# Values in an RWKV-6 kernel: 64 queries with 64 keys for half of the heads, in quarters of the matmul array, and the output's halves by the parity of the pair of heads

## The chip, the cores and the metric

The kernel runs on one core of one Trainium2 chip. The metric is the device time of one execution in microseconds. Five engines work side by side from queues of their own: TensorE (PE, matmuls), VectorE (DVE), ScalarE (ACT), GpSimd (POOL) and SyncE (SP), whose queue issues DMAs.

## The reference

An attention block with a decaying state, and behind it a feed-forward block. All data are float32.

```python
# r, k, v, w: (B=4, H=8, S=768, D=48); u: (H, D)
for t in range(S):
    cur = einsum('bhd,bhe->bhde', u * k[t], v[t])
    y[:, :, t] = einsum('bhd,bhde->bhe', r[t], state + cur)
    state = w[t][..., None] * state + einsum('bhd,bhe->bhde', k[t], v[t])
x = y.transpose(0, 2, 1, 3).reshape(B * S, H * D)       # (3072, 384)
h = x @ w_in                                            # (3072, 2048)
out = (h / (1 + exp(-h))) @ w_out                       # (3072, 384)
```

An output of the attention block is causal: token t takes the state and the keys up to its own, t. In a block of tokens it is therefore a sum of two products: the queries (with the decay up to them) with the state ahead of the block, and the values of the block weighted by scores, which are zero for keys behind the query.

## The kernel before, in words

The sequence is cut into 6 blocks of L = 128 tokens and the batch of 4 into 2 halves of NB = 2. A block with one half of the batch is a unit; there are 12, and they are worked through in order. The 8 heads are 4 pairs p (NP = 4): head 2p + e has its 48 channels in partitions 64 e to 64 e + 47. For the second member of a unit's batch, b = 1, keys and values stand in reversed order along the partitions, for b = 0 in order.

Scores are built in levels. At level l the block is cut into pieces of c = 2^l tokens, and queries of an odd piece meet keys of the even piece before it. `score_products` (L688 to L717) multiplies on TensorE, and VectorE (L722) or ScalarE (L801) puts the result into `score`, laid out as [key, e, b and pair, query]. The part within blocks of 8 tokens is put in by L577, in the units up to index 3 there is L604 for pairs of tokens in its place. The last level, l = 6, lets queries 64 to 127 meet keys 0 to 63. `grow_queries` and `grow_keys` multiply decays into queries and keys between levels.

When a unit's scores are finished, its output y comes from two functions that follow each other on TensorE. `y_state` (L835 to L845) multiplies the 48 x 48 state of each head with 128 queries: for each pair p, each b and each e one product, 16 in all, with rows 64 e of the array and output in partitions 64 b of one of two banks of PSUM, one bank for each e. `y_values` (L847 to L857) runs once for each e: for each p and b it multiplies the 128 x 48 values with the 128 keys by 128 queries of the scores and adds into the same place, 8 products for each e. ScalarE then copies each bank to `yt` in two copies, one for each b (L857). Units 0 and 1 use another function, `y`, which the change leaves alone; so `y_state` and `y_values` run for 10 units.

Behind it `update` (L879) adds the unit's keys and values to the state, and `move_x` moves `yt` by DMAs into `xt`, the layout that the feed-forward block reads. The feed-forward block of earlier units fills TensorE in between: `up` (L987, up-projection and Silu on ScalarE) and `quarter` (L1053, down-projection in seven products of half size by sums and differences that VectorE forms, L1035 and L1062).

The order is written out by hand. `mix` gives groups of attention steps for a unit; the loop at the end of the kernel puts some feed-forward steps behind each group, by the numbers in `room`. The last group of a unit holds the output step:

```python
[(y_state, i), *both(y_values, i), *both(update, i), *at(not ahead, (move_x, i))]
```

From unit 4 on, three up-projections stand between the last score products and this group. TensorE's instructions are in that order in one queue. A product's tile in the array follows from where its operands lie: the rows from the partitions of weights and moving data, the columns from the partitions of the output. A float32 product is carried out as two pairs of weight load and matmul instructions, one after the other in the compiled order.

Of the kernel before, what the change touches and what calls it, by code (L numbers as in the profile page):

```python
# [38 lines left out]
def kernel(  # L39
# [11 lines left out]
    nc = tc.nc  # L51

    B, H, S, D = r.shape
    DM, DF = moe_w_in.shape
    L = 128
    NL = 7
    NB = 2
    NP = H // 2
    PD = 64
# [24 lines left out]
    def bank(name, *dims):  # L84

        have = banks[name][turns_of[name] % 2][:]
        turns_of[name] += 1
        steps, n = [], 1
        for d in dims[::-1]:
            steps.insert(0, [n, d])  # L90
            n *= d
        return bass.AP(tensor=have.tensor, offset=have.offset, ap=[have.ap[0], *steps])
# [4 lines left out]
    vt, vq, whole = {}, {}, {}  # L97
# [191 lines left out]
    state = const.tile([128, B, NP, 2 * PD], F32, name="state")  # L289
# [43 lines left out]
    NSC = 1  # L333
    score = const.tile([128, NSC, 2, Q, L], F32, name="score")

    masks = {}
    first = {}
# [20 lines left out]
    tw, tr, tk, diag, kq, xt = {}, {}, {}, {}, {}, {}  # L358
# [112 lines left out]
    at = 768  # L471
# [358 lines left out]
    p_yt, p_kv, yt = {}, {}, {}  # L830
# [4 lines left out]
    def y_state(i):  # L835

        n, b0 = units[i]
        for e in range(2):
            p_yt[i, e] = bank("p_m", NP, L)
        for p in range(NP):  # L840
            for b in range(NB):
                for e in range(2):
                    rows = slice(PD * e, PD * e + D)
                    nc.tensor.matmul(p_yt[i, e][PD * b:PD * b + D, p, :], lhsT=state[rows, b0 + b, p, rows],  # L844
                                     rhs=tr[i][rows, b * NP + p, :], start=(p == 0), stop=False)  # L845

    def y_values(i, e):  # L847

        for p in range(NP):
            for b in range(NB):  # L850
                at = (2 * p + e) * D
                nc.tensor.matmul(p_yt[i, e][PD * b:PD * b + D, p, :], lhsT=whole[i][b][:, at:at + D],  # L852
                                 rhs=score[:, i % NSC, e, b * NP + p, :], start=False, stop=(p == NP - 1))
        if e == 0:
            yt[i] = pt.tile([128, NP, NB, L], F32, name="yt", bufs=1)
        for b in range(NB):
            nc.scalar.copy(out=yt[i][PD * e:PD * e + D, :, b, :], in_=p_yt[i, e][PD * b:PD * b + D])  # L857

    def y(i, b):

# [64 lines left out]
    def mix(i):  # L925
# [15 lines left out]
        def start(j):  # L941
            return [*[(product, j, l) for l in range(1, NL)], (grow_own, j, 1)]

        end = [[*at(ahead, *bonus_steps(i + 1, 0, 1, 2, 3))],
               [*at(i < len(units) - NB, (turn_apart, i), (turn_k, i)), *at(ahead, *turns(i + 1))],
               [(y_state, i), *both(y_values, i), *both(update, i), *at(not ahead, (move_x, i))]]
        if i < NPAIR:
            groups = [[*both(turn, i, "w"), (product, i, 0)],
# [188 lines left out]
    for m in range(6):  # L1137
# [8 lines left out]
    do((burst, 2, 5), (keep_level, 2, 5), (keep_level, 2, 6), (go_on, 2, 6), (bonus_write, 2), (up, 1, 6), (weight_sums, 1),  # L1146
       (load_values, 3), (turn_apart, 2), (turn_k, 2), (up, 1, 7), (weight_sums, 2), (sums, 1, 2))
    do((sums, 1, 3), (y_state, 2), *both(y_values, 2), *both(update, 2),
       (move_x, 2),
       *blocks[7:])  # L1150
# [44 lines left out]
```

## Time and profile before

| | |
|---|---|
| time, median of 3 runs | 603.54 us (603.06 to 603.57) |
| the profiled execution's own time | 603.03 us |
| its span, first to last instruction | 601.2 us |
| instructions | 15147 |
| matmul instructions | 5982, as many weight loads |
| granted TensorE clock | 1.0 throughout |
| product with the state, L844 | 320 matmul instructions, median 269 ns each |
| values, L852 | 320 matmul instructions, median 273 ns each |
| copies to yt, L857 | 40, median 580 ns each |

The time lies 1.8 us above the span: it takes in what is ahead of the first and behind the last instruction. A matmul's duration is its way from issue to the end of its writes, so matmuls that run behind each other or side by side overlap; what one costs is read from the distance of the starts. The chain that ended last is followed back from the last instruction: at each step to what released it, or to the instruction before it on its engine. "Issue" there is time in which the engine waited for nothing that the profile shows.

### The profile page before, as it was taken

What the parts mean: (1) busy time and instruction counts of PE and PEld (TensorE: products, weight loads), DVE (VectorE), ACT (ScalarE), POOL (GpSimd) and SP (SyncE); (2) the same over time, 40 slices, a digit from 0 to 9 for tenths busy, and PEclk for the clock granted to TensorE, in tenths of its full rate; (3) what the DMA queues carried; (4) which work ended last, traced back from release to release, by engine and by line L of the source; (5) the groups of instructions that cost most, each with busy time, mean ns of one, the idle gap of its engine ahead of it and who ended that gap; (6) DMA issues with size and microseconds to landing.
All of it is one profiled execution on the core that took longest, in us unless ns stands there. A gap on an engine that the chain in (4) does not pass through costs nothing.

```text
span 601.2 us, 15147 instructions
## 1 busy us (share of the span) xinstructions
PE 592.8 (99%) x5982; PEld 529.6 (88%) x5982; DVE 414.9 (69%) x709; ACT 232.5 (39%) x516; POOL 365.1 (61%) x414
## 2 busy tenths in 40 slices
PE   8999999999999999999999999999999999999997
PEld 7787876799899899889889889889889889889997
DVE  6879788798696695596695795686587587551041
ACT  6788883431530530530440351361351242250110
POOL 6998778257678668378578578478578567500000
PEclk9999999999999999999999999999999999999999
DMA  9957793343541643642643643643542531100000
GB/s 218 298 128 201 169 278 48 55 76 49 127 66 54 111 64 52 137 63 51 137 62 54 133 62 54 131 59 53 128 71 50 109 58 27 36 2 27 28 1 26
DMA packets 203079, 53.44 MB, mean 89 GB/s; under 512 B 186752, under 2 KB 194816, under 8 KB 203008
## 3 DMA queue, kind: packets, MB, share of 16 engines
q1 hardware_dynamic: 201424, 51.88, 42.1%
q8 instruction: 47, 0.77, 0.6%
q10 hardware_dynamic: 1584, 0.59, 0.4%
q14 instruction: 24, 0.20, 0.1%
HBM read 43.21 MB, written 5.24 MB: 81 GB/s over the span
## 4 chain that ended last, share of the span: by engine, by line
PE 87%; DVE 4%; POOL 3%; ACT 2%; DMA 1%; issue 1%; SPq 1%; DVEq 0%; POOLq 0%; ACTq 0%
PE p_h L987 38%; PE p_o L1053 34%; PE p_m L852 3%; PE p_m L1009 3%; PE p_sc L704 3%; PE p_m L704 2%; PE p_m L844 2%; POOL tk L645 1%; DMA u_bc<-in_u_dram 1%; DVE score L722 1%; PE p_sc L879 1%; POOL w_out_sb L255 1%; PE p_m L820 1%; POOL tw L422 1%; POOL w_in_sb L255 1%
## 5 line engine op out<-in xcount | busy, mean ns | idle before, releaser
L987 PE MATMUL p_h<-xt,w_in_sb 128*128 128x256 f32 x1152 | 258.9, 382 | 0.8 <-POOL tk L669 0.7
L987 PEld LDWEIGHTS p_h<-xt,w_in_sb 128*128 128x128 f32 x1152 | 215.8, 190 | 31.9 <-POOL tk L669 0.9
L996 ACT ACTIVATE gt<-p_h 128x512 f32<-128x512 f32 x90 | 53.5, 596 | 182.0 <-PE p_h L987 181.7
L645 POOL TENSOR_TENSOR tk<-tk,tw 128x256 f32<-128x256 f32 x128 | 94.2, 757 | 37.3 <-issue 21.4
L1053 PE MATMUL p_o<-own,temps 128*128 128x192 f32 x528 | 88.1, 326 | 0.0
L1053 PE MATMUL p_o<-w_out_sb,gt 128*128 128x192 f32 x508 | 87.4, 328 | 0.0
L1053 PEld LDWEIGHTS p_o<-own,temps 128*128 128x128 f32 x528 | 86.0, 190 | 0.3 <-DVE temps L1062 0.3
L507 POOL TENSOR_TENSOR ruk<-tokens_rk 128x768 f32<-128x768 f32 (+1 forms) x32 | 52.3, 1645 | 53.9 <-DMA tokens_rk<-in_k_dram 21.1
L1053 PEld LDWEIGHTS p_o<-w_out_sb,gt 128*128 128x128 f32 x508 | 82.7, 190 | 0.9 <-issue 0.4
L1035 DVE TENSOR_TENSOR temps<-gt 128x256 f32<-128x256 f32 x84 | 56.2, 669 | 22.4 <-ACT gt L996 22.4
L627 DVE TENSOR_TENSOR tr<-tr,tw 128x512 f32<-128x512 f32 x61 | 54.7, 896 | 16.3 <-PE p_m L704 12.6
L422 POOL TENSOR_TENSOR tw<-tw 128x256 f32<-128x256 f32 (+6 forms) x83 | 43.5, 524 | 36.5 <-DVE tw L374 32.5
L615 ACT COPY tk<-tk 128x256 f32<-128x256 f32 x52 | 21.0, 403 | 102.0 <-POOL tk L645 74.3
L722 DVE COPY_PREDICATED score<-mask,p_sc 128x512 f32<-128x512 int8 x42 | 31.2, 798 | 3.9 <-PE p_sc L704 3.7
L1062 DVE TENSOR_TENSOR temps<-p_o,partial 128x192 f32<-128x192 f32 x22 | 7.9, 358 | 36.1 <-PE p_o L1053 26.8
L1062 DVE TENSOR_TENSOR partial<-p_o,partial 128x192 f32<-128x192 f32 x33 | 11.7, 356 | 28.7 <-PE p_o L1053 28.7
L1035 DVE TENSOR_TENSOR temps<-temps,gt 128x256 f32<-128x256 f32 x43 | 30.4, 706 | 1.5
L1053 PE MATMUL p_o<-w_out_sb,temps 128*128 128x192 f32 x176 | 30.4, 326 | 0.0
L541 DVE TENSOR_REDUCE block_sums<-ruk 128x4 f32<-128x192 f32 (+1 forms) x48 | 24.2, 546 | 7.1 <-POOL ruk L507 7.1
L857 ACT COPY yt<-p_m 48x512 f32<-48x512 f32 x40 | 23.2, 580 | 14.9 <-PE p_m L852 10.1
L1053 PEld LDWEIGHTS p_o<-w_out_sb,temps 128*128 128x128 f32 x176 | 28.9, 190 | 0.0
L704 PEld LDWEIGHTS p_sc<-tr,tk 48*32 48x32 f32 (+1 forms) x1312 | 18.2, 119 | 11.1 <-issue 7.4
(187 smaller groups left out, 841.5 us busy)
## 6 DMA issues: line engine op xcount, KB each, us to landing
w_out_sb<-in_moe_w_in_dram SPq DMA_DIRECT2D x6, 768.0 KB, 6.8
w_out_sb<-in_moe_w_out_dram SPq DMA_DIRECT2D x4, 768.0 KB, 5.7
own<-in_moe_w_out_dram SPq DMA_DIRECT2D x4, 768.0 KB, 5.3
tokens_rk<-in_r_dram SPq DMA_DIRECT2D x8, 384.0 KB, 4.4
tokens_rk<-in_k_dram SPq DMA_DIRECT2D x8, 384.0 KB, 5.3
tokens_w<-in_w_dram SPq DMA_DIRECT2D x8, 384.0 KB, 6.4
xt<-yt SPq DMA_DIRECT2D x60, 48.0 KB, 2.0
raw<-in_w_dram SPq DMA_DIRECT2D x80, 32.0 KB, 1.9
```

Of the source, the lines that this page charges most:

```text
L422: engine.tensor_tensor(out=up, in0=t[:, :, 0::2], in1=t[:, :, 1::2], op=ALU.mult)
L507: mul = lambda out, one, two: nc.gpsimd.tensor_tensor(out=out, in0=one, in1=two, op=ALU.mult)
L541: add = lambda out, have: nc.vector.tensor_reduce(out=out, in_=have, axis=mybir.AxisListType.X, op=ALU.add)
L627: nc.vector.tensor_tensor(out=odd, in0=odd, in1=tw[i][l][:, :, 0::2][:, :, :, None].to_broadcast([128, Q, L >> (l + 1), c]), op=ALU.mult)
L645: nc.gpsimd.tensor_tensor(out=out, in0=have, in1=odd_products(i, l, b, *blocks), op=ALU.mult)
L704: nc.tensor.matmul(to, lhsT=tk[i][rows, X[l % 2] + p, x * m:(x + 1) * m], rhs=have, start=True, stop=True)
L722: nc.vector.copy_predicated(out=dst, mask=masks[l][:, :, None].to_broadcast([128, NB, NP, ni, c]), data=sc[e].rearrange("p (b q) (i c) -> ...
L857: nc.scalar.copy(out=yt[i][PD * e:PD * e + D, :, b, :], in_=p_yt[i, e][PD * b:PD * b + D])
L987: nc.tensor.matmul(p_h[:, a, :], lhsT=w_in_sb[:, c, f * 128:(f + 1) * 128], rhs=xt[i][:, c, :], start=(c == 0), stop=(c == KC - 1))
L996: nc.scalar.activation(out=gt[i, m], in_=p_h, func=AF.Silu)
L1035: nc.vector.tensor_tensor(out=out, in0=one, in1=two, op=op)
L1053: nc.tensor.matmul(p, lhsT=left(f), rhs=right[:, f, :], start=(f == 0), stop=(f == FH - 1))
```

## The change

It touches `y_state` and `y_values` alone, and adds a helper that names the place of an output.

First, places. The output of head (p, e) of member b was in partitions 64 b of bank e, at slot p of four. Now it is in partitions 64 (p % 2) of bank e, at slot (p // 2) 2 + b. The loop over the state products keeps its order p, b, e; with the place, the column half of the array that a product uses changes from b to p % 2.

Second, values. For the heads with e = b, the first 64 queries can meet only 64 of the keys: those in partitions 0 to 63 for b = 0, and, reversed, those in 64 to 127 for b = 1. These parts, 64 keys by 64 queries for each of the 4 pairs and both b, become 8 products of their own behind the state products in `y_state`; each uses the row half b and the column half p % 2. In `y_values` the same heads take only queries 64 to 127 with all 128 keys. The other heads are as before. The loop there is now b outside, p inside.

Third, the copies follow the new places: one for each parity x of the pair, with pairs x and x + 2 and both b.

```diff
                     rows = slice(PD * e, PD * e + D)
-                    nc.tensor.matmul(p_yt[i, e][PD * b:PD * b + D, p, :], lhsT=state[rows, b0 + b, p, rows],
-                                     rhs=tr[i][rows, b * NP + p, :], start=(p == 0), stop=False)
-
-    def y_values(i, e):
-
+                    nc.tensor.matmul(y_place(i, e, p, b), lhsT=state[rows, b0 + b, p, rows],
+                                     rhs=tr[i][rows, b * NP + p, :], start=(p < 2 and b == 0), stop=False)
+
+        half = L // 2
         for p in range(NP):
             for b in range(NB):
+                rows, at = slice(b * half, (b + 1) * half), (2 * p + b) * D
+                nc.tensor.matmul(y_place(i, b, p, b)[:, 0:half], lhsT=whole[i][b][rows, at:at + D],
+                                 rhs=score[rows, i % NSC, b, b * NP + p, 0:half], start=False, stop=False)
+
+    def y_place(i, e, p, b):
+
+        x = p % 2
+        return p_yt[i, e][PD * x:PD * x + D, p // 2 * NB + b, :]
+
+    def y_values(i, e):
+
+        for b in range(NB):
+            first = L // 2 if b == e else 0
+            for p in range(NP):
                 at = (2 * p + e) * D
-                nc.tensor.matmul(p_yt[i, e][PD * b:PD * b + D, p, :], lhsT=whole[i][b][:, at:at + D],
-                                 rhs=score[:, i % NSC, e, b * NP + p, :], start=False, stop=(p == NP - 1))
+                nc.tensor.matmul(y_place(i, e, p, b)[:, first:], lhsT=whole[i][b][:, at:at + D],
+                                 rhs=score[:, i % NSC, e, b * NP + p, first:], start=False, stop=(b == NB - 1 and p >= NP - 2))
         if e == 0:
             yt[i] = pt.tile([128, NP, NB, L], F32, name="yt", bufs=1)
-        for b in range(NB):
-            nc.scalar.copy(out=yt[i][PD * e:PD * e + D, :, b, :], in_=p_yt[i, e][PD * b:PD * b + D])
+        for x in range(2):
+            nc.scalar.copy(out=yt[i][PD * e:PD * e + D, x::2, :, :],
+                           in_=p_yt[i, e][PD * x:PD * x + D].rearrange("p (q b) t -> p q b t", b=NB))
```

## The prediction

> **What bounds the kernel now.** I read the page's engine shares first, then the chain that ended last, then the pieces of that chain in order of time, then the starts of single TensorE instructions. The page gives the shares of the span of 601.2 us and the shares of the chain:
>
> ```profile
> PE 592.8 (99%) x5982; PEld 529.6 (88%) x5982; DVE 414.9 (69%) x709; ACT 232.5 (39%) x516; POOL 365.1 (61%) x414
> PE 87%; DVE 4%; POOL 3%; ACT 2%; DMA 1%; issue 1%; SPq 1%; DVEq 0%; POOLq 0%; ACTq 0%
> ```
>
> TensorE is busy all the time, and the chain runs through it for 87%. A busy share alone could hide waits, so I look at the chain in order of time around one unit's output step (start, length, what):
>
> ```profile
> 444.01 0.63 PE p_m L820 x16
> 444.64 2.79 PE p_h L987 x12
> 447.43 1.02 PE p_m L844 x32
> 448.45 1.88 PE p_m L852 x32
> 450.34 0.72 PE p_sc L879 x32
> 451.05 18.40 PE p_o L1053 x112
> 469.45 0.62 PE p_sc L704 x32
> ```
>
> Each piece begins where the one before it ends, all on TensorE. From 90 us, well before the first product with the state at 121 us, to 598 us the chain has no piece of another engine, and the units repeat every 46.4 us with the same lengths. So a TensorE nanosecond saved inside this stretch is a nanosecond of the end. The two pieces that the change touches are L844 (product with the state, 1.02 us) and L852 (values, 1.88 us), 2.90 us in each of 10 units.
>
> The waits agree. What stands before L844 and L852 is called issue, that is, no other engine is waited for:
>
> ```profile
> PEld p_m L844 <- issue: 3.0, 9, 0.3
> PEld p_m L852 <- issue: 1.9, 10, 0.2
> ```
>
> Next, how these pieces are made. The timeline of TensorE over one unit (start, us, line, what; the first line stands for 32 instructions):
>
> ```profile
> 537.72 1.09 PE L844 MATMUL p_m<-tr,state 48*48 48x128 f32 x32
> 538.74 0.31 PE L852 MATMUL p_m<-score,vt 128*48 128x128 f32 x1
> 538.75 0.31 PE L852 MATMUL p_m<-score,vq 128*48 128x128 f32 x1
> 538.89 0.27 PE L852 MATMUL p_m<-score,vt 128*48 128x128 f32 x1
> 538.90 0.27 PE L852 MATMUL p_m<-score,vq 128*48 128x128 f32 x1
> 539.00 0.27 PE L852 MATMUL p_m<-score,vt 128*48 128x128 f32 x1
> 539.00 0.27 PE L852 MATMUL p_m<-score,vq 128*48 128x128 f32 x1
> ```
>
> Every float32 product is two matmul instructions (16 products, x32). L852 starts in pairs, one in each half of the columns; the trace's starts are 109 ns apart from pair to pair. L844 starts in fours, one in each quarter: 537.721, .728, .735, .741, then .868, .977, 538.086 and so on, again 109 ns a step. So L844 is 8 steps of four (0.873 us) and L852 is 16 steps of two (1.746 us), and each piece carries some 0.14 us more for filling the array and draining it before the next layout of tiles.
>
> In the compiled order the two instructions of one product follow each other, yet the second vt starts after the first vq. So a waiting instruction lets one for another tile pass. This matters below.
>
> **What the Trainium skill says.** TensorEngine Tiling (Array Packing), Key Properties: tiles work in parallel, and changing the tiling mode drains the engine. The trace agrees: 109 ns inside a piece, about 0.2 us from the last start of L844 to the first of L852. TensorE: Matmul & The Clock Gate, Back-to-back issue gap: time follows the number of moving columns, N/2.4 ns plus a floor; the trace has twice that slope for float32 (109 ns for 128 columns). The same page, "What overlaps and what doesn't", says matmuls start in program order; the vt, vq order above contradicts it across tiles, and the measurement decides. How many waiting instructions can be passed is shown by no run here.
>
> **The change part by part.** (1) Price of a 64-column step. The last score level has products of exactly the new kind, 64-column, in quarters:
>
> ```profile
> 484.31 0.69 PE L704 MATMUL p_m<-tr,tk 48*64 48x64 f32 x32
> ```
>
> Its eight groups of four start at 484.307, .414, .472, .531, .589, .647, .706 and .764: the first step takes 107 ns, the others 58.4. For two tiles of 128 rows the nearest row is the state update L879 with 48 columns, 45 ns a step by its starts; 10 ns above that for 16 more columns gives 55 to 60, so I take 58.4 there too. A 64-column step saves 109.1 - 58.4 = 50.7 ns.
>
> (2) Removed from the values: for each of the two e, the 4 heads with b = e take 64 columns instead of 128. That is 8 of 16 products, 16 of 32 instructions, 8 of 16 steps of two: 8 x 50.7 = 0.406 us a unit less.
>
> (3) Added behind the product with the state: 8 products of 64 x 48 weights and 64 columns, 16 instructions, in tiles (row half b, column half p % 2). Their order p, b visits all four quarters in turn, as L704 does: 4 steps of 58.4 = 0.234 us more. They use the same 64 x 64 tiles as L844, so they add no drain; a drain, if the step from 48 to 64 rows caused one, would cost about 0.14 us a unit. They could hide below 0.234 only in quarters that the state product leaves idle, and full steps of four leave none.
>
> (4) First instructions. The values' first step is now a 64-column one, 107 instead of 148 ns: 41 rather than 50.7 saved, 0.01 us of the sum in (2). The drain behind the last step stays at 0.11 us.
>
> (5) Moved: the state products. Their count and columns stay, but the column half is now p % 2 and the loop is still p, b, e. Before, four consecutive products fell into four quarters. Now four consecutive products fall into two quarters of one column half, each twice, and the next four into the other half. Each quarter still gets 4 products, 8 instructions, so the work is 8 full steps if later instructions may pass four waiting ones in each tile. I take zero, because passing is seen, though not at this depth: in L704's 32-column level, at 483.722, a weight load goes past waiting instructions of four other tiles. The other end is in the rivals.
>
> (6) Waits. The quarter products read scores about 0.9 us after the first state product, where the values read them 1.02 us after it. The last score writer ends 4.9 us ahead of the product with the state in the last two units, 5.7 to 7.2 us in those before, and 1.3 us in the first, so this waits for nothing. Were that cover gone, up-projections queued behind on TensorE would be late by the overrun. No DMA issue is added or moved.
>
> (7) The copies L857 keep 48 rows of 512 elements, 580 ns each; runs of 256 instead of 128 on the output side. ScalarE is 39% busy, and its next user of the result, the move to xt, feeds an up-projection some 18 us later, behind the 18.40 us of L1053. Nothing.
>
> Sum per unit: +0.234 - 0.406 + 0.01 = -0.162 us. Ten units: -1.62 us, say 1.6. The profiled execution took 603.03 us with a span of 601.2, so it would be 601.4 with a span of 599.6. The median of the runs shown, 603.54, is 0.5 higher; it goes to **601.9 us**, 0.27% faster. A measurement of this kernel can tell about 0.2%, 1.2 us, from no change.
>
> **The rivals.** *The gain is partly eaten in the array (same).* The queue in front of each quarter is short. If a quarter holds one running and two waiting instructions, the fourth of the four holds back the other column half until a step has passed, the halves run one step apart, and the block ends one step (0.109 us) later; the gain falls to 0.05 us a unit, 603.0. If it holds one running and one loaded, two steps are lost (0.218), the balance is +0.06 a unit, 604.1. A drain between 48 and 64 rows (0.14) would give 603.3. For it: only one waiting instruction per tile is plainly visible in the traces. Against: the passing at L704, over four tiles at once. Taken at 603.3.
>
> *The fours fall into pairs (slower).* Place: the state product. If no instruction of the second column half starts before the eight of the first half's group are nearly done, 8 steps of four become 16 of two: 8 x 0.109 = 0.873 us a unit more, balance +0.71, ten units +7.1: 610.6 us. It decides from 1.5 lost steps a unit on, where the gain of 0.162 is gone, and is outside the 0.2% from 2.6 lost steps on. For it: the source order now has pairs. Against: the vt, vq starts, and loads that begin 41 ns behind the first ones, while the tile still streams.
>
> *The time saved is not the end's (same).* Something waits in place of TensorE, 603.5. Against: no other engine in the chain for ten units, VectorE at 69%, GpSimd at 61%. For it: only that GpSimd's bonus work waits for its DMAs.
>
> **How the numbers follow.** Full gain 0.60 (601.9, own range 601.3 to 602.4, from the bounds of the 64-column step and the spread of the runs); partly eaten 0.20 (603.0 to 604.1); pairs 0.13 (610.6, or in between); not the end's 0.07. Of the first, 0.02 falls short of 0.2%; of the second, about 0.01 passes it on the slow side. Faster 0.58, same 0.28, slower 0.14. The range goes from 601.2 to 604.2: it takes in the eaten cases and leaves out the pairs and the tails.
>
> **What would show it.** Right: L844's piece with the quarter products about 1.25 us with 48 matmuls, of which the new ones step by 58 ns in fours; L852 about 1.49 us; starts in fours over both column halves from the first step on; the period of a unit 46.2 us. Wrong: state products starting in twos, or a gap of 0.1 us or more between state and quarter products; a second drain; a wait for the score copies L801 ahead of the quarter products; or a chain that leaves TensorE between 121 and 598 us.

## The result and the profile after

The kernel after takes 601.52 us (median of 11 runs), the kernel before 603.04 in the runs beside it. The ratio is 0.9975, 95% interval 0.9967 to 0.9983: 1.5 us faster. The profiled execution took 601.21 us with a span of 599.4, where before it was 603.03 and 601.2.

The page of the kernel after, engine shares and shares of the chain:

```profile
PE 591.4 (99%) x6142; PEld 529.8 (88%) x6142; DVE 415.2 (69%) x709; ACT 232.8 (39%) x516; POOL 363.6 (61%) x414
PE 87%; POOL 5%; DVE 4%; ACT 3%; issue 1%; POOLq 0%; DVEq 0%; ACTq 0%
```

There are 160 more matmul instructions, 8 products x 2 x 10 units, and TensorE is 1.4 us less busy. It is still what the chain runs through. The chain in order of time around one unit (start, length, what; L851 is the quarter products, L865 the values, L893 the update that was L879):

```profile
399.91 1.06 PE p_m L844 x32
400.97 0.23 PE p_m L851 x15
401.20 1.46 PE p_m L865 x32
402.65 0.72 PE p_sc L893 x32
403.37 18.40 PE p_o L1067 x112
```

State, quarters and values take 1.06 + 0.23 + 1.46 = 2.75 us, where it was 1.02 + 1.88 = 2.90. All else in the unit is as before, and from unit to unit the first state products are now 46.200 us apart instead of 46.364. Between the first of the ten units and the second nothing was gained: 47.956 us, where it was 47.951. The reason stands under "The bound" below. Nine times 0.164 is 1.5 us, which is the gain of the medians. The two spans differ by 1.8 us; 0.26 of this lies ahead of the first product with the state (at 120.890 instead of 121.150 us), where nothing was changed.

How the pieces are made, from the timeline of TensorE in the next unit (a quarter of the array is a 64 x 64 tile: one half of the rows and one half of the columns):

```profile
446.04 1.13 PE L844 MATMUL p_m<-tr,state 48*48 48x128 f32 x32
446.95 0.22 PE L851 MATMUL p_m<-score,vt 64*48 64x64 f32 x1
446.96 0.22 PE L851 MATMUL p_m<-score,vq 64*48 64x64 f32 x1
447.00 0.22 PE L851 MATMUL p_m<-score,vt 64*48 64x64 f32 x1
...
447.33 0.43 PE L865 MATMUL p_m<-score,vt 128*48 128x64 f32 x8
```

The quarter products start in one column half at 446.95 and in the other at 447.00. The halves are 50 ns apart, because the last state products ahead of them are (446.844 and 446.894). The first starts of the state products are at 446.043 and 446.049 in one half, 446.069 and 446.076 in the other, so all four quarters run from the beginning. The first values start 1.283 us behind the first state product.

For the sums below I use the distance between first starts in the traces, over the units with an update, where each repeats within 2 ns:

| us a unit | before | after |
|---|---|---|
| first state product to first values | 1.021 | 1.283 |
| first values to first update | 1.785 | 1.358 |
| sum | 2.806 | 2.641 |

### The profile page after: what moved, and what is told of

The parts are those of the page before. It is cut to its first block, busy times and chain, and to the rows that moved or that the text cites. A ratio compares the mean times of both kernels' runs of the same rounds, so it can differ in the third digit from the quotient of the medians.

```text
span 599.4 us, 15477 instructions
## 1 busy us (share of the span) xinstructions
PE 591.4 (99%) x6142; PEld 529.8 (88%) x6142; DVE 415.2 (69%) x709; ACT 232.8 (39%) x516; POOL 363.6 (61%) x414
## 4 chain that ended last, share of the span: by engine, by line
PE 87%; POOL 5%; DVE 4%; ACT 3%; issue 1%; POOLq 0%; DVEq 0%; ACTq 0%
PE p_h L1001 38%; PE p_o L1067 33%; PE p_m L1023 3%; PE p_sc L704 3%; PE p_m L865 2%; PE p_m L844 2%; PE p_m L704 2%; POOL w_in_sb L255 1%; POOL tk L645 1%; PE p_sc L893 1%; POOL w_out_sb L255 1%; DVE score L722 1%; PE p_m L820 1%; POOL tw L422 1%; DVE p_w L242 1%
## 5 line engine op out<-in xcount | busy, mean ns | idle before, releaser
L507 POOL TENSOR_TENSOR ruk<-tokens_rk 128x768 f32<-128x768 f32 (+1 forms) x32 | 51.0, 1606 | 55.8 <-DMA tokens_rk<-in_k_dram 40.2
L1049 DVE TENSOR_TENSOR temps<-gt 128x256 f32<-128x256 f32 x84 | 57.8, 688 | 22.4 <-ACT gt L1010 22.4
L627 DVE TENSOR_TENSOR tr<-tr,tw 128x512 f32<-128x512 f32 x61 | 52.6, 862 | 18.0 <-PE p_m L704 14.3
L1049 DVE TENSOR_TENSOR temps<-temps,gt 128x256 f32<-128x256 f32 x43 | 32.3, 752 | 1.5
L898 POOL TENSOR_TENSOR state<-state,tw 128x512 f32<-128x512 f32 x16 | 21.9, 1386 | 10.3 <-PE p_m L844 10.3
```

What stands on the lines that cost most here:

```text
L507: mul = lambda out, one, two: nc.gpsimd.tensor_tensor(out=out, in0=one, in1=two, op=ALU.mult)
L627: nc.vector.tensor_tensor(out=odd, in0=odd, in1=tw[i][l][:, :, 0::2][:, :, :, None].to_broadcast([128, Q, L >> (l + 1), c]), op=ALU.mult)
L1049: nc.vector.tensor_tensor(out=out, in0=one, in1=two, op=op)
```

## The experiments

Each time is a median. The ratio is to runs of the kernel before that were made beside it, with its 95% interval.

**The places alone.** The quarter products go, the values take all 128 queries, the new places and orders stay.

```diff
-        half = L // 2
-        for p in range(NP):
-            for b in range(NB):
-                rows, at = slice(b * half, (b + 1) * half), (2 * p + b) * D
-                nc.tensor.matmul(y_place(i, b, p, b)[:, 0:half], lhsT=whole[i][b][rows, at:at + D],
-                                 rhs=score[rows, i % NSC, b, b * NP + p, 0:half], start=False, stop=False)
...
-            first = L // 2 if b == e else 0
+            first = 0
```

> Only the new places and loop orders, without the quarter products; the values take all 128 queries again. It isolates the moved state products. My theory (waiting instructions of four in a row are passed, no step is lost): state block 1.02 us as before, values 1.78 to 1.79, the time of before within 0.2 us, ratio 1.000. Rival, gain partly eaten in the array: one or two steps lost a unit, 1.1 to 2.2 us slower than before. Rival, fours fall into pairs: 8.7 us slower.

603.2 us, ratio 1.0002 (0.9992 to 1.0012). The chain of this kernel, L858 being the values:

```profile
447.17 1.06 PE p_m L844 x32
448.22 1.88 PE p_m L858 x32
```

The state block is 1.057 us instead of 1.021, the values 1.784 as before. No step of 0.109 is lost, but 0.036 us is: the order of the state products has a small price, which I had at nothing.

**The column half by b again.** The quarter products stay, but reach only two quarters.

```diff
     def y_place(i, e, p, b):
-        x = p % 2
-        return p_yt[i, e][PD * x:PD * x + D, p // 2 * NB + b, :]
+        return p_yt[i, e][PD * b:PD * b + D, p, :]
```

The loop of the values is p, b again, and the copies and flags follow the place.

> The quarter products kept, but the column half follows b again as before, so that a quarter product with row half b and column half b reaches two of the four quarters only. My theory (the quarter products cost their steps): 8 steps of two instead of 4 of four, 0.47 us instead of 0.23, against 0.43 saved in the values: 0.3 to 0.9 us slower than before, some 2.3 us slower than the change. Rival, that the quarter products hide beside other work: as fast as the change, 1.5 us faster than before.

603.7 us, ratio 1.0011 (0.9997 to 1.0025), which can't be told from no change; the span is 0.6 us longer than before and 2.4 us longer than after. Its chain:

```profile
447.80 1.02 PE p_m L844 x32
448.82 0.45 PE p_m L851 x16
449.26 1.46 PE p_m L864 x24
```

The quarter products take 0.45 us instead of 0.23, and the values are 0.42 us shorter than before (1.46 for 1.88): in two quarters they cost more than they save. They are not hidden behind anything; it is the parity of the pair that brings them into four quarters.

**The quarter products behind the values.**

The six lines move out of `y_state`, and the end of `y_values` becomes:

```diff
+        if e == 0:
+            return
+        half = L // 2
+        for p in range(NP):
+            for b in range(NB):
+                rows, at = slice(b * half, (b + 1) * half), (2 * p + b) * D
+                nc.tensor.matmul(y_place(i, b, p, b)[:, 0:half], lhsT=whole[i][b][rows, at:at + D],
+                                 rhs=score[rows, i % NSC, b, b * NP + p, 0:half], start=False, stop=(p >= NP - 2))
+        for e in range(2):
             for x in range(2):
```

> The same quarter products, but behind the values of both e instead of behind the state products, and all four copies behind them. The work in each kind of tile is that of the change, with two more changes of the tile layout in each of the 8 units that update the state behind it and one more in the last two. My theory (a change of layout drains the array and costs 0.11 to 0.15 us): 18 more, 2.0 to 2.7 us slower than the change, so 0.5 to 1.2 us slower than before. Rival, that the place is indifferent: 1.5 us faster than before, as the change.

603.95 us, ratio 1.0010 (1.0002 to 1.0018). The same products as in the change, and the gain is gone:

```profile
448.35 1.06 PE p_m L844 x32
449.41 1.46 PE p_m L858 x32
450.87 0.37 PE p_m L868 x16
451.24 0.85 PE p_sc L895 x32
```

L868, the quarter products, takes 0.37 instead of 0.23, and the update L895 0.85 instead of 0.72. A unit is 46.480 us, 0.280 more than with the change, for two more changes of the tile layout: 0.14 each. From the last but one unit to the last, where no update follows and only one change is added, it is 0.18 (44.833 us instead of 44.655). That they stand behind the product with the state, in its layout, is worth the whole gain.

**The state products in turn.** As the change, with the loop visiting the four quarters one after the other. This loop and the orders further down are written here as nested loops; the kernels have the same orders as one list.

```diff
-        for p in range(NP):
-            for b in range(NB):
-                for e in range(2):
+        for q in range(0, NP, 2):
+            for b in range(NB):
+                for p in (q, q + 1):
+                    for e in range(2):
```

> The change with the state loop in the order that visits the four quarters in turn (pairs of the same parity group by group). The trace of the change shows fours, but the second column half starts 27 ns behind the first and later 51 ns. My theory (that lag is all that the order costs): 0.02 to 0.03 us a unit, 0.2 to 0.3 us less than the change, block with the quarter products 1.25 to 1.26 us instead of 1.28. Rival, that the order costs a step: 1.1 us less than the change.

601.45 us, ratio 0.9973 (0.9963 to 0.9982). The times can't tell it from the change. The trace can: the first values start 1.246 us behind the first state product instead of 1.283, in every unit, and a unit is 46.160 us instead of 46.200.

```profile
445.70 1.02 PE p_m L844 x32
446.72 0.23 PE p_m L851 x16
```

**Eight in a row, and quarter by quarter.** Two orders of the state products that ask how many waiting instructions can be passed: eight in a row for each quarter of one column half, then the other half; and one quarter of the array after the other.

```diff
+        for x in range(2):
+            for p in (x, x + 2):
+                for b in range(NB):
+                    for e in range(2):
```

```diff
+        for x in range(2):
+            for e in range(2):
+                for p in (x, x + 2):
+                    for b in range(NB):
```

> The change with the state loop taking one column half to its end before the other: sixteen instructions for two quarters, then sixteen for the other two, so eight waiting in each quarter instead of four. It asks how deep the passing goes. My theory (what waits is held in one queue of some 32 pairs, and any tile's next instruction may be taken from it): still fours, the second half starts about 53 ns behind the first, 0.3 to 0.6 us slower than the change. Rival, the queue ahead of a tile is short, so that eight in a row hold back the other half: 0.3 to 0.87 us a unit, 3 to 8.7 us slower than the change.

> The change with the state loop taking one quarter of the array after the other, eight instructions each: the first instruction of the last quarter is the 25th pair of load and matmul. My theory (one queue of some 32 pairs): quarters start 27 ns apart, the last 80 ns late, 0.5 to 1.0 us slower than the change in ten units. Rival, short queues for each tile: the product falls to ones and twos, up to 24 steps more, several us to 26 us slower.

605.81 us, ratio 1.0047 (1.0034 to 1.0060), and 615.52 us, ratio 1.0210 (1.0193 to 1.0226): 4.3 and 14 us slower than the change, with the same instructions. My theory of one queue of some 32 pairs, from which any tile's next may be taken, falls. The state products at the head of their chains, first half by half, then quarter by quarter:

```profile
449.57 1.16 PE p_m L844 x25
```

```profile
455.86 2.10 PE p_m L844 x29
```

The starts show the rule. With eight in a row, the second half of the array starts 487 ns behind the first, 13 ns behind the *fifth* instruction of the first half. Quarter by quarter, each quarter starts 6 ns behind the fifth instruction of the quarter ahead. At the fifth start, four of the eight have made way, one runs and three wait: the eighth has just found room. The rule that fits: a quarter holds four matmul instructions, one running and three behind, and one for which there is no room stops the queue for all quarters.

**Six in a row**, to test that rule on another number.

```diff
+        for part in (((0, 0), (0, 1), (2, 0)), ((2, 1),)):       # (pair, b)
+            for x in range(2):
+                for e in range(2):
+                    for p, b in [(q + x, b) for q, b in part]:
```

> The change with six matmul instructions in a row for each quarter of one column half, then six for the other, then two each. The two runs with eight in a row show the other half starting with the fifth instruction of the first: each quarter holds four, one running and three behind, and the next one stops the queue for all. My theory from that: the second column half starts with the third step of the first, about 0.26 us behind it, and the block with the quarter products takes 1.47 to 1.51 us, 2.0 us more than the change in ten units. Rival, a common limit of 16 or 32 waiting instructions: the second half would start 0.02 to 0.05 us behind, or 0.37 as with eight in a row.

608.54 us, ratio 1.0086 (1.0070 to 1.0101). By the rule the sixth finds room when the third starts, and so each quarter should start with the third instruction of the quarter ahead. That is what the trace has. My expected time is off all the same, 2.0 us where it is some 7 slower than the change: I let the first two quarters start together, but their order is one after the other too, so the second column half waits for two such holds, 0.52 us, and the fourth quarter for three. Starts in ns from the first state product of a unit, from the traces:

```
                    2nd quarter   3rd      4th      instruction ahead that starts just before
after                     6       26       33       (none: four in a row fit)
eight in a row            6      487      493       5th of the 1st half: 474
quarter by quarter      480      960     1440       5th: 474, 954, 1434
six in a row            261      523      785       3rd: 256, 517, 779
```

The common limit of 16 or 32 waiting instructions gives none of these numbers. Nor does any other limit that all quarters share: when the next quarter starts, three instructions wait in quarter by quarter, but six, three in each of two quarters, in eight in a row.

**Without the quarter products**, to price them alone.

The edit takes out the same six lines as the first experiment; the values keep their 64 queries for the heads with e = b.

> The change without the quarter products: the first 64 queries of half of the heads get no values, which leaves out part of the computation. It prices the quarter products alone. My theory: four steps of about 58 ns a unit and the lag of the second half, 0.22 to 0.27 us, so 2.2 to 2.7 us faster than the change, 3.8 to 4.3 faster than before. Rival, they hide in the drain: under 1 us.

599.7 us, ratio 0.9946 (0.9933 to 0.9959): 3.3 us less than before and 1.8 less than the change. State and values take 2.416 us a unit instead of 2.641, so the quarter products cost 0.225. They are not hidden. But the first of the ten units gains nothing here either (47.980 us to the next one), so this counts nine times, 2.0 us. The spans differ by 1.8, since this execution reached its first state product 0.2 us later. The expected gain of 2.2 to 2.7 us over the change counted ten units.

**One change of layout less.** On top of the state products in turn, in units 4 to 9 the key transposes L820 go directly ahead of the state product; first with the output step one up-projection earlier, then with the transposes one later.

```diff
+        if NPAIR <= i < len(units) - NB:
+            end[1:] = [end[1] + end[2], []]       # the first run
+            end[1:] = [[], end[1] + end[2]]       # the second
```

The transposes use the banks p_sc in these units.

> The change with the state loop in turn, and in units 4 to 9 the key transposes put directly ahead of the state product (in the other two PSUM banks) instead of one up-projection earlier, so that one change of the tile layout between them and the up-projections goes in each of these 6 units. My theory (a change of layout costs 0.11 to 0.15 us): 0.7 to 0.9 us less than with the state loop in turn alone, 600.6. Rival, that the wait for the copies of the keys ahead of the state update takes its place: no gain or a loss.

> As the key transposes ahead of the state product, but in units 4 to 9 the third up-projection goes ahead of both, so the output step stays where it was and the transposes and the work behind them come 2.8 us later. In the run before, five units were 0.20 us shorter each, and the first of them lost 2.6 us to a late DMA into xt. My theory (that loss came from the output step moving ahead): no such loss, 1.0 to 1.2 us less than with the state loop in turn alone, near 600.3. Rival, the later turns make VectorE and GpSimd late instead: a wait of TensorE ahead of the scores, no gain.

601.94 us, ratio 0.9987 (0.9976 to 0.9998), and 601.53, ratio 0.9973 (0.9963 to 0.9984). Neither beats the state loop in turn alone. One change of layout less is worth what was said and more: where nothing waits, a unit is 45.963 us instead of 46.160, so 0.20 less. (It is a balance: two changes, into and out of the up-projection, went, and one, from transposes to state products, came.) But other units pay it back. In the first kernel one unit loses to a wait for xt's DMA. In the second two units are 46.62 and 46.87 us long, one with a shorter wait for the same DMA, the other with a wait for VectorE:

```profile
PE p_h L1003 <- DMA xt<-yt: 2.2, 1, 2.2
```

```profile
PE p_h L1003 <- DMA xt<-yt: 0.4, 1, 0.4
PEld p_o L1069 <- DVE partial L1078: 0.9, 1, 0.9
```

The traced execution of the first kernel took 605.5 us, so the size of that loss is not the median's. In the second, those two units are 1.2 us longer together than with the state products in turn, and the other four 0.8 us shorter. Why two units of six come late and the others don't stays open; the chain ahead of the wait for VectorE goes through the load of the next decays (DMA into raw), GpSimd and VectorE.

## Why the prediction was right

**The bound.** TensorE alone, with no other engine in the chain while the ten units run: right for nine of the ten units. Orders that made a unit longer moved the time by about ten times what they added on TensorE, up to 14 us. In the first unit it was wrong. There the chain after leaves TensorE for VectorE, which the prediction had named as a sign of being wrong:

```profile
124.42 5.33 PE p_o L1067 x32
129.75 1.18 DVE tk L374 x2
...
132.15 0.37 DVE temps L1076
```

The down-projection waits for a sum that VectorE forms only behind transposes of keys and queries. The chain before shows this stretch as TensorE alone, but the wait was there, once, and could be read from the waits before; the second line is from after:

```profile
PEld p_o L1053 <- DVE temps L1062: 0.3, 1, 0.3
PEld p_o L1067 <- DVE temps L1076: 0.4, 1, 0.4
```

By the timelines it grew from 0.27 to 0.44 us, by what TensorE had saved in that unit. The kernels with the state products in turn (47.976 us to the next unit) and without the quarter products (47.980) gained nothing there either. So the sum below counts nine times: -1.5 us, where the prediction had -1.6. Its 601.9 stood on a median of 603.54; from the 603.04 of the runs beside the change, nine units give 601.6, and 601.52 was measured.

**The sum.** Predicted -0.162 us a unit, measured -0.165. That it came so close is luck: its terms were off by -0.031, -0.009 and +0.036, which cancel.

| step of the prediction | predicted | measured | from |
|---|---|---|---|
| (2) and (4), values | -0.396 | -0.427 | 1.785 to 1.358 |
| (3), quarter products | +0.234 | +0.225 | with and without them, 2.641 - 2.416 |
| (5), state products moved | 0 | +0.036 | the places alone, 1.057 - 1.021 |
| sum | -0.162 | -0.166 | |

In (2) the 64-column steps in two tiles take 56 ns (the starts after: 447.419, .475, .531, .587) where I took 58.4 from steps in four tiles with 64-column weights, and the first takes 93 instead of 107. In (3) they are 55 to 60 ns, as read from L704. The drain of 0.11 us behind the values in (4) is none: the update stands in the same layout, and its first start follows the values' last one by one step, 110 ns before and 56 after. For the same reason the values carried 0.04 us beyond their steps before, not some 0.14. The sum does not change with it.

**Step (5)** was right in its conclusion and wrong in its reason. I argued from passing over one waiting instruction in each of four tiles, and supposed passing deeper. What holds is a limit of four for each quarter, and the change happens to put exactly four in a row into each, which the prediction could not know. It just fits, and not quite: in the trace of the change the fifth weight load of the second column half starts at 446.528 instead of at about 446.436, once the first half's fifth instruction has started at 446.517 and its eighth has found room. The second half is 50 instead of 26 ns behind from there on. With the products in turn nothing of this is left. So of the extra 0.036 us the hold has 0.024; the other 0.013 is there from the first start, where the second half comes 26 and 33 ns behind the first product instead of 14 and 20. The run in turn takes away both at once; the division is read from the starts alone.

**The rival of the partly eaten gain** was the same mechanism with three or two places for each quarter. It has four, and the hold costs some 0.02 us a unit, not 0.11. **The pairs** did not come with four in a row; with eight they do, 0.44 us a unit rather than 0.87, since the halves still overlap by four steps. **The drain** between 48 and 64 rows did not come: the quarter products follow the last state products at their step. **Time that is not the end's** came in one unit of ten, as said above, and the last two runs show that it lies near elsewhere: a reordering by 2.8 us is enough to make a DMA or VectorE late.

**Waits, DMAs, copies** at nothing: right for the scores, the DMAs and the copies, and wrong for the one wait for VectorE; the issue waits ahead of L844 are 3.0 us in 9 of the units as before, and the chain has no wait for the copies L801 ahead of L851.

## What to carry to other kernels

Small products side by side in the array are priced by steps: count how many of them are in the same tile, how many columns a step has, and how often the layout changes (0.14 to 0.18 us here). Put extra products where their layout already stands, and spread them over all tiles: that alone decided here between 1.5 us faster and no gain (0.6 and 0.9 us slower by the medians, the first of them not clear of noise). Let the order of issue visit the tiles in turn; more than four matmul instructions in a row for one quarter leave the others idle. Before a saving is multiplied by the number of units, read the waits in each unit's stretch: where the engine already waits for another one, even 0.3 us, a saving only makes that wait longer.

## What the runs showed of the hardware that I had not expected

- Matmuls start out of program order across tiles, but only as long as there is room: a 64 x 64 quarter held four float32 matmul instructions, one running and three behind, and the next one stopped the queue for every quarter. Orders of four, six and eight in a row gave starts of the next quarter at once, with the third and with the fifth instruction, to within 13 ns. No number that all quarters share fits both the order by quarters (three waiting) and the order by halves (six).
- The same 16 products of a state block, in five orders and with the quarter products behind them, took 1.246, 1.283, 1.720, 2.011 and 2.667 us up to the first values.
- A change of the tile layout among small products cost 0.14 us (0.280 for two in a unit); taking an up-projection out from between transposes and state products, one change less on balance, saved 0.20 us.
